# Four small matmuls in TensorE's first waits, and a recomposed work list, in a fused attention and SwiGLU kernel

## The chip, the core and the metric

The kernel runs on one NeuronCore of one Trainium2 chip. The metric is the device time of one execution in microseconds (us); lower is better. Four runs of the kernel before gave 371.88 to 372.51 us with a median of 372.19 us.

## What is computed

Attention over 8 batches of 8 heads, 576 positions of width 64, with 16 extra "beacon" keys and values per head ahead of the ordinary ones. Its output, with the heads side by side, is the input of a SwiGLU feed-forward block on 4608 tokens.

```python
k_all, v_all = concat([beacon_k, k]), concat([beacon_v, v])    # 592 keys
scores = q @ k_all.T / 8 ; scores[ordinary key later than the query] = -1e9
x = softmax(scores) @ v_all                      # to 4608 x 512
g = x @ w_gate ; val = x @ w_val                 # 512 -> 1536
out = (g * sigmoid(g) * val) @ w_out             # 1536 -> 512, fp32 out
```

Inputs and output are fp32; inside, the operands of TensorE are bf16, and the loads on GpSimd's DMA queue convert as they copy.

## The kernel before

**Attention** goes by batch `b` and pair of heads `m` (4 pairs a batch). For one pair the scores of all keys against all queries are cut into four units, A, B, C and D, of 496, 464, 496 and 208 columns for each of the two heads; a unit's matmuls fill a PSUM tile of the pool `big` (3 buffers, `scores`, L285), ScalarE takes the exponent into the tile `p` (L260), and the causal triangle is cut out in one of three ways. Letter `e` in the work list: GpSimd's affine_select on `p` after the exponent (L268). Letter `d`: a multiplication with a 0/1 tile on VectorE (L264). Letter `s`: a matmul that adds -30000 to the scores on TensorE before the exponent (`mask_on_pe`, L249). Units A, B and D take one such GpSimd or VectorE instruction each, C two; with `s` the number doubles, one for each head. `P` is the product with the values for one head, 15 matmuls (`pv`, L309), and two VectorE instructions that normalise it into `x`.

**Queries and keys** must be transposed. Batch 0 is loaded in another layout and regrouped by copies (`c` on VectorE, `C` on GpSimd), then transposed by TensorE: `K`, `Q` with the copy out of PSUM on VectorE, `k`, `q` with it on ScalarE. Batches 1 and 2 are transposed by TensorE too (`U`, `u`, L228); the later ones by DMA from SyncE's queue (`t`, ten a batch). The attention output of batch 0 is transposed by TensorE (`X`, `x`), that of the others by DMA as soon as a batch's last `P` is issued.

**The feed-forward block** goes by chunks `j` of 512 tokens. `G` is one unit of 128 hidden columns: 8 matmuls of 512 columns (L354), Tanh on ScalarE (L367) and two VectorE instructions (L369, L372). The first three units of chunk 0 are cut into nine parts `g`, so that they can begin before all of batch 0 is there. `F` is one matmul of 512 columns of the output projection (L393; twelve make a tile of 128 tokens, which VectorE copies out and SyncE stores).

**Loads.** `l` issues the next of 125 loads of values, keys and queries in a fixed order (`loads`), `w` the next of 8 weight loads of 384 KB (`weights`: gate and value weights for hidden units 0-2, 3-5, 6-8, 9-11), `o` the next half of `w_out`, 768 KB. All of them go through GpSimd's queue, on the same engine as the masks `e`. Each load uses one of eight semaphores in turn, so that a load is issued only when the eighth before it has landed.

**The work list** `plan` sets the order. It is one long string; every letter calls `piece`, which issues that piece to its engines. An engine executes its own instructions in exactly this order, so a TensorE instruction that waits holds all later matmuls, and a mask that waits on GpSimd holds all later loads. Assertions in `piece` state what a piece needs.

**At the start** VectorE zeroes the first 512 columns of one `p` tile, and TensorE runs 15 matmuls on them into a spare PSUM tile (`warm`, L467: nine of 512 columns, six of 128) while the first loads come in.

Of the kernel before, what the change touches and what calls it, by code (L numbers as in the profile page):

```python
# [14 lines left out]
P = 128  # L15
S = 576
# [4 lines left out]
TOK = 512  # L21
# [38 lines left out]
def kernel(  # L60
# [65 lines left out]
    def load_runs(t, src, h0, h1):  # L126
# [151 lines left out]
    def scores(burst):  # L278

        tiles = [big.tile([P, 2, 512], FP32, name="s_ps", tag="big") for _ in burst]  # L280
        for (b, m, u, mask), ps in zip(burst, tiles):
            for t, col, q0, n in UNITS[u][2]:
                for hh in range(2):
                    r = slice(64 * hh, 64 * hh + 64)
                    nc.tensor.matmul(  # L285
                        ps[:, hh, col : col + n],
                        lhsT=kT[b % 2][r, m, P * t : P * t + P],
                        rhs=qT[b % 2][r, m, q0 : q0 + n],
                        start=mask != "s" or col == 0,
                        stop=mask != "s",  # L290
                    )
            if mask != "s":
                exponent(b, m, u, mask, ps)
# [136 lines left out]

    nc.vector.memset(pt[1][:, 0, 0:TOK], 0.0)
    for eng, t, src in ((nc.sync, first_k, k), (nc.scalar, first_q, q)):
        eng.dma_start(t[:].rearrange("p (h e) -> p h e", h=2), src[0, 0:2].rearrange("h (p i) d -> p h (i d)", i=ROWS))
    nc.sync.dma_start(beacons_in[:], beacon_k[0].rearrange("h j d -> j h d"))
# [28 lines left out]
    def warm(n, cols):  # L465
        for _ in range(n):
            nc.tensor.matmul(  # L467
                idle[:, 0:cols], lhsT=pt[1][:, 0, 0:P], rhs=pt[1][:, 0, 0:cols], start=True, stop=True
            )

    warm(9, TOK)
# [19 lines left out]

    done = dict.fromkeys("SPKQUXgGFltwoc", 0)
    first = [[(0, 0, 2), (1, 0, 2), (0, 2, 3), (1, 2, 3), (2, 0, 2), (2, 2, 3), (0, 3, 4), (1, 3, 4), (2, 3, 4)]]
    parts = [(j, *part) for j in range(len(first)) for part in first[j]]
    units = [(j, f) for j in range(NCH) for f in range((3, 0)[min(j, 1)], NF)]
# [28 lines left out]
    def piece(kind):  # L526
# [48 lines left out]
            projection.pop(0)()  # L575
        elif kind == "o":
            load_wo(n)
        elif kind == "w":
            weights[n]()
        elif kind in "cC":  # L580
# [11 lines left out]
    one_bank = [(outp, "outp")]  # L592
    two_banks = [(outp, "outp"), (att, "att")]
    plan = [
        "lllllllclQkcKeeQcdscwCwKeslcQssQKsswPwPeePPewXee",
        "XPllsPgPxgllPwggXlllgwlgwogggGGllGGGGoGlGulGFddF",
        "lllFFFFUddlllllFlFlFllFlFFUdeFFFPUlddlPFFdeeFFFF",
        "PFllFlFdePeeFFlPuFFlllPdeeFFPueFPFdeFlFFtFUeeFFF",
        "PFlFdeelPFtUePtFFeeFPFdeelFPFlllGllGGPtGtGlllGlG",
        "lllPGlGGGllGllllFlFFltttttedFPlFFteetFFFFtFFeeel",  # L600
        "PFtllFFFFFtPddeFtFPFFltFFledePllFFFFFFdddFllFltF",
        "FltPGGPlGtFllGtlPFGtGGGtGGlPttGllFddFllFFFFFlFdt",
        "eeFFFtFlGFddFPtlFFFFdeeFtFFtFlFFPdleeFFFFlFFFlFP",
        "FFeleldPFFGlGttFtFGFGlFFFFPFFFllldeeFPFtGFFeePFF",
        "FdeetFFFPFlGlGGFtGGlFtPFGGlGFlFllFFFFFPFtFldeePF",
        "FFGPGFFFlFlFlFteeFFFFeteelFPFGlteldFFFFPFFGFFFFG",
        "tFlFGGFFFFFFFPFeeleFFFFPGGtGGFFFteeFFFPlFFtFleed",
        "tFFFGGPGFGtGPlGFFtFFdeFFFFFPFFeeetlPFFtGGGFFFFFF",
        "FFFFPeddFFFFPFFlFdedFFFFFPGGGFFFFFFlFeeFFFFFPeee",
        "FFFFFFPFFFFFFPeedFFFFFFFFFFPdeeFFPGFFFGPGGFGFPFG",  # L610
        "GPFFGFGFGFFGGFFFFFFFFFFFFFGFFFFGFFFFGFGFFFFFFFFF",
        "FFFFFGGFFFFGGGGFFFFGGFFFFFFFFFFFFFGFFGFFFFFGFFFG",
        "FFFFFFFGFFFFFFFGFGFFFFFGFGGFFGFGFFFFFFFFFFFFFFFF",
        "FFFFFFFFFFFFFFFFFFFFFFFFFFFFFFFFFFFFF",
    ]
    for kind in re.findall("[sde]{3}(?![sde](?![sde]))|[sde]{1,2}|.", "".join(plan)):
        piece(kind)
    assert done == dict(S=16 * B, P=8 * B, K=4, Q=4, U=4 * (NPE - 1), X=4 * NPEX, g=9, G=len(units), F=4 * NF * NCH, w=8, o=2, c=6, l=len(loads), t=len(turns)), done


# [28 lines left out]
```

The softmax here doesn't subtract the row's maximum and nothing guards it: scores larger than these inputs give would overflow.

## Time and profile before

| | |
|---|---|
| median of four runs | 372.19 us |
| the profiled execution's own time | 371.94 us |
| its span | 370.2 us |
| TensorE busy (matmuls) | 358.3 us, 97% |
| VectorE, ScalarE, GpSimd busy | 241.0, 171.3, 149.6 us |
| TensorE idle before a named wait of over 0.15 us | 1.3 + 1.3 + 0.9 + 0.8 + 0.4 + 0.4 + 0.3 + 0.2 + 0.2 us and 0.7 us of "issue" |

The span starts at 0 with the first instruction of the program; the time beside it has 1.74 us more. A matmul of 512 columns starts 0.216 us after the one before (eight in 1.73 us), though the row of one says 379 ns: the rows overlap, because matmuls are pipelined. "Idle before, and releaser" tells how long the engine had nothing to do before an instruction and what ended that. PEclk is the share of TensorE's full clock that was granted.

### The profile page before, as it was taken

The page shows a single profiled execution, that of the slowest core. Times are in us where ns is not written, and L with a number is a line of the kernel's source. Part 1 is how long each engine was busy: PE and PEld are TensorE (multiplying, and loading weights), DVE is VectorE, ACT ScalarE, POOL GpSimd, SP SyncE. Part 2 cuts the span into 40 slices and gives each one's busy share as a digit, 9 for nine tenths or more (in the row PEclk, how much of TensorE's full clock was granted, in tenths as well). Part 3 has the DMA queues.
Part 4 walks back from the last instruction along what each step waited for, and adds up shares of the span by engine and source line. Part 5 has one row for each costly group of instructions (what it writes and reads, how often), then busy time and mean ns, then how long its engine had stood idle before and what let it go on. Part 6 is the DMA issues. An engine that isn't in the chain of part 4 may idle for free.

```text
span 370.2 us, 7227 instructions
## 1 busy us (share of the span) xinstructions
PE 358.3 (97%) x2792; PEld 180.7 (49%) x2839; DVE 241.0 (65%) x474; ACT 171.3 (46%) x245; POOL 149.6 (40%) x251
## 2 busy tenths in 40 slices
PE   7998999999989999999999999999999999999996
PEld 3663455654444445454454444544555444444443
DVE  5758776768746875666855766767367746656662
ACT  3853379953475258464265454544642311311210
POOL 8987479886768515828045212121310000000000
PEclk9699999999999999999999999999999999999999
DMA  9999999999999999999949178136200301001003
GB/s 167 131 187 176 200 171 154 112 168 115 153 120 162 164 170 138 154 187 92 171 63 109 48 110 120 40 52 93 81 30 0 92 31 57 2 29 57 30 30 112
DMA packets 160978, 39.61 MB, mean 107 GB/s; under 512 B 149040, under 2 KB 156464, under 8 KB 160944
## 3 DMA queue, kind: packets, MB, share of 16 engines
q0 software_dynamic: 112304, 18.83, 73.1%
q1 hardware_dynamic: 48432, 20.02, 27.8%
q8 instruction: 22, 0.36, 0.4%
q10 hardware_dynamic: 208, 0.29, 0.3%
q14 instruction: 12, 0.10, 0.1%
HBM read 38.27 MB, written 9.44 MB: 129 GB/s over the span
## 4 chain that ended last, share of the span: by engine, by line
PE 79%; DMA 12%; POOL 3%; issue 2%; ACT 1%; DVE 1%; POOLq 0%; ACTq 0%
PE gv_ps L354 42%; PE o_ps L393 22%; PE pv_ps L309 6%; PE s_ps L285 6%; DMA qb<-in_q_dram 4%; DMA wo<-in_moe_w_out_dram 3%; DMA wg<-in_moe_w_gate_dram 2%; DMA vb<-in_v_dram 1%; POOL qb L137 1%; ACT p L260 1%; DMA first_k<-in_k_dram 1%; POOL kb L137 1%; PE t_ps L204 1%; PE o_ps L413 1%; PE t_ps L228 1%
## 5 line engine op out<-in xcount | busy, mean ns | idle before, releaser
L367 ACT ACTIVATE th<-gv_ps 128x512 f32<-128x512 f32 x108 | 64.4, 597 | 150.7 <-PE gv_ps L354 138.2
L260 ACT ACTIVATE p<-s_ps 128x992 bf16<-128x992 f32 (+2 forms) x128 | 101.8, 865 | 28.2 <-PE s_ps L285 26.4
L369 DVE SCALAR_TENSOR_TENSOR u<-th,gv_ps 128x512 f32<-128x512 f32 x108 | 74.2, 687 | 62.1 <-ACT th L367 60.6
L354 PE MATMUL gv_ps<-xT,wg 128*128 128x512 bf16 x419 | 110.5, 379 | 2.1 <-DVE hT L372 1.3
L354 PE MATMUL gv_ps<-xT,wv 128*128 128x512 bf16 x425 | 111.0, 379 | 0.4
L393 PE MATMUL o_ps<-wo,hT 128*128 128x512 bf16 x393 | 103.8, 380 | 1.7 <-issue 0.5
L372 DVE SCALAR_TENSOR_TENSOR hT<-gv_ps,u 128x512 bf16<-128x512 f32 x108 | 74.7, 691 | 3.7
L268 POOL TENSOR_SCALAR_AFFINE_SELECT p<-p 128x256 bf16<-128x256 bf16 (+2 forms) x101 | 37.4, 395 | 97.9 <-ACT p L260 91.9
L354 PEld LDWEIGHTS <-wv 128*128 128x128 bf16 x432 | 42.2, 98 | 51.1 <-DMA wv<-in_moe_w_val_dram 0.4
L354 PEld LDWEIGHTS <-wg 128*128 128x128 bf16 x432 | 41.2, 98 | 47.8 <-issue 1.7
L393 PEld LDWEIGHTS <-hT 128*128 128x128 bf16 x420 | 37.2, 98 | 44.0 <-issue 7.0
L309 PEld LDWEIGHTS <-p 128*128 128x128 bf16 x960 | 36.5, 97 | 13.3 <-DVE x L318 1.4
L309 PE MATMUL pv_ps<-vb,p 128*128 128x65 bf16 x960 | 39.9, 193 | 1.4 <-DMA vb<-in_v_dram 0.9
L137 POOL DMA_DIRECT2D vb<-in_v_dram x40 | 34.1, 862 | 9.1 <-DMA qb<-in_q_dram 6.0
L285 PE MATMUL s_ps<-qT,kT 64*128 64x80 bf16 (+4 forms) x384 | 34.0, 290 | 0.8 <-DMA qT<-qb 0.3
L318 DVE TENSOR_TENSOR x<-pv_ps,rec 128x320 bf16<-128x320 f32 x64 | 31.5, 492 | 2.3
L137 POOL DMA_DIRECT2D qb<-in_q_dram x35 | 30.2, 863 | 4.9 <-PE gv_ps L354 2.2
L137 POOL DMA_DIRECT2D kb<-in_k_dram x35 | 30.0, 858 | 4.4 <-DMA wo<-in_moe_w_out_dram 1.7
L402 DVE COPY o_sb<-o_ps 128x512 f32<-128x512 f32 x35 | 24.0, 685 | 10.4 <-PE o_ps L393 10.3
L264 DVE TENSOR_TENSOR p<-p,upper 128x256 bf16<-128x256 bf16 (+2 forms) x49 | 13.7, 296 | 22.5 <-ACT p L260 22.2
L285 PEld LDWEIGHTS <-kT 64*128 64x128 bf16 x384 | 14.1, 95 | 18.5 <-issue 11.4
L317 DVE RECIPROCAL rec<-pv_ps 128x5 f32<-128x5 f32 x64 | 12.1, 189 | 15.7 <-PE pv_ps L309 15.5
(55 smaller groups left out, 84.5 us busy)
## 6 DMA issues: line engine op xcount, KB each, us to landing
out_dram<-o_sb SPq DMA_DIRECT2D x35, 256.0 KB, 2.2
qb<-in_q_dram POOLq DMA_DIRECT2D x28, 128.0 KB, 7.3
vb<-in_v_dram POOLq DMA_DIRECT2D x24, 128.0 KB, 5.5
kb<-in_k_dram POOLq DMA_DIRECT2D x21, 128.0 KB, 6.7
wg<-in_moe_w_gate_dram POOLq DMA_DIRECT2D x4, 384.0 KB, 7.9
wv<-in_moe_w_val_dram POOLq DMA_DIRECT2D x4, 384.0 KB, 9.0
wo<-in_moe_w_out_dram POOLq DMA_DIRECT2D x2, 768.0 KB, 12.8
vb<-in_v_dram POOLq DMA_DIRECT2D x8, 112.0 KB, 5.2
```

Source lines behind the costliest of these rows:

```text
L137: return eng.dma_start(dst[p0 : p0 + n, c, h0:h1, 0:D], src[b, h0:h1, r : r + n, :].rearrange("h j d -> j h d"))
L260: nc.scalar.activation(p[:, :, c0 : c0 + w], ps[:, :, 0:w], ACT.Exp, scale=0.125)
L268: nc.gpsimd.affine_select(out=ap, in_=ap, compare_op=ALU.is_ge, fill=0.0, base=d, pattern=[[0, 2], [1, n]], channel_multiplier=-1,)
L285: nc.tensor.matmul(ps[:, hh, col : col + n], lhsT=kT[b % 2][r, m, P * t : P * t + P], rhs=qT[b % 2][r, m, q0 : q0 + n], start=mask != "s" ...
L309: nc.tensor.matmul(o_ps[:, c, 0 : D + 1], lhsT=pt[(NPAIR * b + m) % NPT][:, hh, col : col + P], rhs=vb[b % 2][:, t, h, 0 : D + 1], start=( ...
L318: nc.vector.tensor_tensor(out=xs[b][:, :, D * h : D * h + D], in0=o_ps[:, :, 0:D], in1=rec[:].to_broadcast([P, NKT, D]), op=ALU.mult,)
L354: nc.tensor.matmul(gvs[f][:, TOK * half : TOK * half + TOK], lhsT=w[:, kk, P * f : P * f + P], rhs=xT[:, kk, r : r + TOK], start=(kk == 0) ...
L367: nc.scalar.activation(th[:], ps[:, 0:TOK], ACT.Tanh, scale=0.5)
L369: nc.vector.scalar_tensor_tensor(out=u[:], in0=th[:], scalar=1.0, in1=ps[:, 0:TOK], op0=ALU.add, op1=ALU.mult)
L372: nc.vector.scalar_tensor_tensor(out=hTs[j][:, f, :], in0=ps[:, TOK:1024], scalar=0.5, in1=u[:], op0=ALU.mult, op1=ALU.mult)
L393: nc.tensor.matmul(st["o"][:], lhsT=hTs[j][:, f, P * i : P * i + P], rhs=wo[:, f, :], start=(f == 0), stop=(f == NF - 1),)
L402: nc.vector.tensor_copy(o_sb[:], st["o"][:])
```

## The change

- A new letter `h`, four times in the list. While at most two score units have been issued it is a `warm` matmul of 256 columns into the spare PSUM tile; later it is remembered in `heat` and issued at the head of the next burst of scores, into that burst's own first tile, ahead of its first score matmul, which overwrites it. Three of the four are of the first kind, one of the second.
- The zeros lie in `p` tile 2 instead of 1.
- The whole list is another one. It has the same pieces with these differences: for batch 0's first pair the two transposes are `q`, `k` (both copied out by ScalarE) and the second pair's keys too (`k`), where it was `Q`, `k`, `K`; all six regroupings are on VectorE (one was on GpSimd).
- The masks: 28 matmuls on TensorE (20 before), 60 instructions on VectorE (49), 86 on GpSimd (101).
- The loads of weights and inputs interleave otherwise: the first gate weights go out right behind batch 1's first key block, the second half of `w_out` ahead of batch 1's values, and so on.

```diff
@@ -129,6 +129,7 @@
             src[0, h0:h1].rearrange("h (p i) d -> p h (i d)", i=ROWS),
         )
 
+    heat = []
     loaded = {}
 
     def rows(eng, dst, src, b, h0, h1, c, p0, r, n):
@@ -278,6 +279,11 @@
     def scores(burst):
 
         tiles = [big.tile([P, 2, 512], FP32, name="s_ps", tag="big") for _ in burst]
+        while heat:
+            heat.pop()
+            nc.tensor.matmul(
+                tiles[0][:, 0, 0 : 2 * P], lhsT=pt[2][:, 0, 0:P], rhs=pt[2][:, 0, 0 : 2 * P], start=True, stop=True
+            )
         for (b, m, u, mask), ps in zip(burst, tiles):
             for t, col, q0, n in UNITS[u][2]:
                 for hh in range(2):
@@ -430,7 +436,7 @@
 
 
 
-    nc.vector.memset(pt[1][:, 0, 0:TOK], 0.0)
+    nc.vector.memset(pt[2][:, 0, 0:TOK], 0.0)
     for eng, t, src in ((nc.sync, first_k, k), (nc.scalar, first_q, q)):
         eng.dma_start(t[:].rearrange("p (h e) -> p h e", h=2), src[0, 0:2].rearrange("h (p i) d -> p h (i d)", i=ROWS))
     nc.sync.dma_start(beacons_in[:], beacon_k[0].rearrange("h j d -> j h d"))
@@ -465,7 +471,7 @@
     def warm(n, cols):
         for _ in range(n):
             nc.tensor.matmul(
-                idle[:, 0:cols], lhsT=pt[1][:, 0, 0:P], rhs=pt[1][:, 0, 0:cols], start=True, stop=True
+                idle[:, 0:cols], lhsT=pt[2][:, 0, 0:P], rhs=pt[2][:, 0, 0:cols], start=True, stop=True
             )
 
     warm(9, TOK)
@@ -491,7 +497,7 @@
 
 
 
-    done = dict.fromkeys("SPKQUXgGFltwoc", 0)
+    done = dict.fromkeys("SPKQUXgGFltwoch", 0)
     first = [[(0, 0, 2), (1, 0, 2), (0, 2, 3), (1, 2, 3), (2, 0, 2), (2, 2, 3), (0, 3, 4), (1, 3, 4), (2, 3, 4)]]
     parts = [(j, *part) for j in range(len(first)) for part in first[j]]
     units = [(j, f) for j in range(NCH) for f in range((3, 0)[min(j, 1)], NF)]
@@ -575,6 +581,12 @@
             projection.pop(0)()
         elif kind == "o":
             load_wo(n)
+        elif kind == "h":
+            assert done["S"] < 8
+            if done["S"] <= 2:
+                warm(1, 2 * P)
+            else:
+                heat.append(1)
         elif kind == "w":
             weights[n]()
         elif kind in "cC":
@@ -592,29 +604,30 @@
     one_bank = [(outp, "outp")]
     two_banks = [(outp, "outp"), (att, "att")]
     plan = [
-        "lllllllclQkcKeeQcdscwCwKeslcQssQKsswPwPeePPewXee",
-        "XPllsPgPxgllPwggXlllgwlgwogggGGllGGGGoGlGulGFddF",
-        "lllFFFFUddlllllFlFlFllFlFFUdeFFFPUlddlPFFdeeFFFF",
-        "PFllFlFdePeeFFlPuFFlllPdeeFFPueFPFdeFlFFtFUeeFFF",
-        "PFlFdeelPFtUePtFFeeFPFdeelFPFlllGllGGPtGtGlllGlG",
-        "lllPGlGGGllGllllFlFFltttttedFPlFFteetFFFFtFFeeel",
-        "PFtllFFFFFtPddeFtFPFFltFFledePllFFFFFFdddFllFltF",
-        "FltPGGPlGtFllGtlPFGtGGGtGGlPttGllFddFllFFFFFlFdt",
-        "eeFFFtFlGFddFPtlFFFFdeeFtFFtFlFFPdleeFFFFlFFFlFP",
-        "FFeleldPFFGlGttFtFGFGlFFFFPFFFllldeeFPFtGFFeePFF",
-        "FdeetFFFPFlGlGGFtGGlFtPFGGlGFlFllFFFFFPFtFldeePF",
-        "FFGPGFFFlFlFlFteeFFFFeteelFPFGlteldFFFFPFFGFFFFG",
-        "tFlFGGFFFFFFFPFeeleFFFFPGGtGGFFFteeFFFPlFFtFleed",
-        "tFFFGGPGFGtGPlGFFtFFdeFFFFFPFFeeetlPFFtGGGFFFFFF",
-        "FFFFPeddFFFFPFFlFdedFFFFFPGGGFFFFFFlFeeFFFFFPeee",
-        "FFFFFFPFFFFFFPeedFFFFFFFFFFPdeeFFPGFFFGPGGFGFPFG",
-        "GPFFGFGFGFFGGFFFFFFFFFFFFFGFFFFGFFFFGFGFFFFFFFFF",
-        "FFFFFGGFFFFGGGGFFFFGGFFFFFFFFFFFFFGFFGFFFFFGFFFG",
-        "FFFFFFFGFFFFFFFGFGFFFFFGFGGFFGFGFFFFFFFFFFFFFFFF",
-        "FFFFFFFFFFFFFFFFFFFFFFFFFFFFFFFFFFFFF",
+        "lllllllclchqwkhhkescQdshcKcelseQcwKswQelswPPdweP",
+        "PessXXlsPPwwgPxllllglPglgwXggglggoGGGGGGGoGlulll",
+        "lGFdldFFFFllFUllddlFlFlFFUesFFPdldllFlFlePlUeFFP",
+        "ddslFPFFFleeFPFFFllsPlUFPFleeFPtltUdFFFlFddeFFtl",
+        "FPtUeeFFPUdelFPltFdlFFFFPFtdelllFltFFPddelttlFll",
+        "lFPlGGllGGGGPGGltPGlGGGFFlleelFtltFFtFFeetFltFll",
+        "llFFFlllleeeFFlFFtFFFedtlFFFlFeeFGGllGPFFFlGtFFP",
+        "GGPtGeeFFFlPlltlFFFFeelePFFGtPGlFFdetFFFFFtPFddl",
+        "elFFPGGltPGFddFFFFFPtlddeFFlFlllFttPFFeeePFFFFtF",
+        "FdedFFtFFGlGtFGtPlFGlGlPlGeeFFFPtFFtlFdeteFPFFtF",
+        "ddFlFlGtltGlGlFtFFGGFlFFFFFFlFFetePlGGFFFeelFFFF",
+        "FFPdtdeFFFGFPFFGFedlFFPFFFledeFFPFGtPFFGFGlGPFFl",
+        "tGFFFFFFtFGlPFFFlllFFFFdedFFFFFGPGGFttFFFeeFFPFe",
+        "eelPFFFFFGeePFFFFFFtttFFdddFFFlFtGtGlGFFFFPGPFFF",
+        "FFFFFGdeFFFFFFPlFFdedPFFlGGFGFGGGlFFeeFFFFFFFPFF",
+        "FedePFFFFFFFedeFFFFPFGPGFFFFFFFPFeddFFFFPGGPGFFF",
+        "FFFPFFFGGGFFFGGGGFFFFFFFFFFFFGFFFFGFFGFGFFFFGFFF",
+        "GFFGFFGFFFFFFGFFFFGGFGFFFFFFFFFFFGFFFFFGFFFFFGFF",
+        "FFFFFGFFFGFFGFGFGFFFFFFGFFFFFFFGFFGFFGFFFFFFFFFF",
+        "FFFFFFFFFFFFFFFFFFFFFFFFFFFFFFFFFFFFFFFFF",
     ]
     for kind in re.findall("[sde]{3}(?![sde](?![sde]))|[sde]{1,2}|.", "".join(plan)):
         piece(kind)
+    del done["h"]
     assert done == dict(S=16 * B, P=8 * B, K=4, Q=4, U=4 * (NPE - 1), X=4 * NPEX, g=9, G=len(units), F=4 * NF * NCH, w=8, o=2, c=6, l=len(loads), t=len(turns)), done
 
 
```

## The prediction

> **What bounds the kernel.** I read the page's busy times first, then TensorE's waits, then the clock by stretches.
>
> ```profile
> PE 358.3 (97%) x2792; PEld 180.7 (49%) x2839; DVE 241.0 (65%) x474; ACT 171.3 (46%) x245; POOL 149.6 (40%) x251
> ...
> PE gv_ps L354 <- DVE hT L372: 1.3, 1, 1.3
> PE idle_ps L467 <- DVE p L433: 1.3, 1, 1.3
> PE pv_ps L309 <- DMA vb<-in_v_dram: 0.9, 2, 0.6
> PE t_ps L204 <- DVE qb L193: 0.8, 1, 0.8
> ...
> PE o_ps L393 <- DMA wo<-in_moe_w_out_dram: 0.4, 1, 0.4
> PE t_ps L201 <- DVE qT L193: 0.4, 1, 0.4
> ...
> ```
>
> TensorE is the bound: a microsecond saved anywhere else counts only if TensorE waited for it. All its named waits come to 6.5 us, so the prize is small. The second place to look is how fast TensorE ran while it was busy.
>
> ```profile
> core 0: us, PE busy (x) PEld busy (x) DVE busy (x) ACT busy (x) POOL busy (x), PEclk, DMA share, GB/s
> ...
> 4.73:8.14 3.41, 2.25 (x30) 1.53 (x30) 2.54 (x7) 1.52 (x4) 3.27 (x7) 1.00 1.29 189
> 8.14:11.55 3.41, 3.41 (x31) 1.85 (x29) 2.48 (x7) 3.02 (x4) 3.41 (x6) 0.50 2.06 158
> 11.55:14.97 3.42, 3.42 (x33) 2.21 (x29) 2.04 (x6) 2.79 (x5) 3.42 (x6) 0.50 1.86 113
> ...
> ```
>
> From 8.14 to 14.97 us the granted clock was half. The stretch before it holds the two waits at 5.41 us (0.77) and 7.15 us (0.39), which is where three of the four new matmuls go.
>
> **Part 1: the four matmuls.** A 512-column matmul takes 0.216 us from start to start at full clock, so 256 columns take 0.11, 0.21 at half clock. One lies in the 0.77 us wait for the query regrouping, two (0.22) in the 0.39 us wait for the first query copy: hidden, cost 0. Without that cover they would cost 0.33. The fourth stands in the second wave of scores, with no wait named before it: 0.1 to 0.2 us, taken as 0.1.
>
> **Part 2: does the clock stay up?** At most, half of the 6.83 us at half clock comes back, 3.4 us, but ScalarE caps it. Its rows:
>
> ```profile
> 7.19 0.72 ACT L191 ACTIVATE kT<-t_ps 128x16 bf16<-128x16 bf16 x2 [1.15 <-PE t_ps L204]
> 8.53 3.14 ACT L260 ACTIVATE p<-s_ps 128x992 bf16<-128x992 f32 x4 [0.62 <-PE s_ps L285]
> 11.92 1.83 ACT L260 ACTIVATE p<-s_ps 128x992 bf16<-128x992 f32 x2 [0.25 <-PE s_ps L285]
> 14.14 1.41 ACT L260 ACTIVATE p<-s_ps 128x416 bf16<-128x416 f32 x2 [0.38 <-PE s_ps L249]
> 16.16 6.22 ACT L260 ACTIVATE p<-s_ps 128x992 bf16<-128x992 f32 x8 [0.62 <-PE s_ps L249]
> ```
>
> Batch 0's exponents are 12.6 us of work and end at 22.38. The last three gaps between them (0.25 + 0.38 + 0.62 = 1.25 us) are all that a faster TensorE can close. Against that, the second pair's key copy (0.72, as the row at 7.19) now stands on ScalarE ahead of the first exponent. By my order: queries' copy 6.66 to 7.32 (0.66, the ScalarE row of 576 columns), keys' to 8.04, second keys' to 8.76; the first exponent starts at 8.76 instead of 8.53, 0.23 late. Kept clock: 1.25 - 0.23 = 1.0 us earlier at best. Lost clock: 0.2 late.
>
> Here the Trainium skill is to be weighed ("TensorE: Matmul & The Clock Gate", Part 1): the gate looks at windows of about 3.4 us, a busy one opens it, an idle one halves the clock. The windows are here (3.41 us each). But the stretch at 4.73 was busy for 2.25 of 3.41 us and closed the gate all the same, and the one at 8.14 was recorded as busy throughout and did not open it. The page's Part 4 says that transposes don't count as busy in the same way; with that, what counts in the stretch at 4.73 is the tail of the warm-up alone, about 0.5 us, and the three matmuls make 0.85. By the general rule (a gap below 3.4 us keeps the clock) the gain would be 1.0; by the row, that a nearly full stretch did not open it, nothing. The page also says that the windows run free, so that their place may differ from run to run. I take 0.4 us of gain, nearer to the middle than to either end, and keep -1.0 to +0.2.
>
> A second cap: hidden unit 9 of chunk 0 needs the last value weights. They were issued at 31.8 us and landed 9.2 us later, at 41.0; TensorE started those matmuls at 41.06. In both lists this load has the same loads ahead of it, so TensorE can't be earlier there than the queue is. GpSimd's rows show room:
>
> ```profile
> 12.20 0.89 POOL L268 TENSOR_SCALAR_AFFINE_SELECT p<-p 128x224 bf16<-128x224 bf16 x2
> 13.04 0.77 POOL L166 DMA_DIRECT2D wg<-in_moe_w_gate_dram  x1
> 13.80 0.84 POOL L193 COPY kb<-ks 96x768 bf16<-96x768 bf16 x1
> 14.57 0.76 POOL L166 DMA_DIRECT2D wv<-in_moe_w_val_dram  x1
> ```
>
> Two masks and a copy stand between the loads, and from 14.5 to 15.5 us only 30 GB/s moved, against 141 to 195 around it. The new list sends the first gate weights at 12.2 and has the copy on VectorE; up to 0.8 us earlier landings follow. So 0.4 is allowed.
>
> **Part 3: the late waits.**
>
> ```profile
> 49.53 0.81 PE L393 MATMUL o_ps<-wo,hT 128*128 128x512 bf16 x3 [0.41 <-DMA wo<-in_moe_w_out_dram]
> ...
> 99.56 0.37 PE L285 MATMUL s_ps<-qT,kT 64*128 64x464 bf16 x2 [0.34 <-DMA qT<-qb]
> ...
> 104.75 0.31 PE L309 MATMUL pv_ps<-vb,p 128*128 128x65 bf16 x5 [0.64 <-DMA vb<-in_v_dram]
> 105.31 0.19 PE L309 MATMUL pv_ps<-vb,p 128*128 128x65 bf16 x1 [0.24 <-DMA vb<-in_v_dram]
> ```
>
> *w_out.* Its second half was issued at 36.1, behind a beacon block and one block of batch 1's values, and landed at 49.5. Now only the beacon block is ahead; landings in this stretch are 0.65 to 0.9 us apart, so it lands about 0.7 earlier, at 48.8, where TensorE asked from 49.1. Gain 0.4. The values behind it end where they did (52.9), and the first `P` of batch 1 asks at 52.6 for its first block: no slack to spare, but no new load.
>
> *Transposed queries of batch 3.* I laid both lists out in TensorE's own work (G 1.73, F 0.216, P 0.56, a pair's scores about 0.7 us). Before, the last five DMA transposes stood directly ahead of batch 3's first scores. Now the last one stands 8 us ahead; one took 6.5 us to land at 92 us. Gain 0.34. What its data need, batch 3's last query block, was issued at 81.7; its letter now comes 3 us earlier.
>
> *Values of batch 3.* The first `P` stood 4 us behind the letter of the last value block, now 10 us. That block landed 4.9 us after its issue at 100.4. Gain 0.64 + 0.24 = 0.88.
>
> Sum: 1.6 us. The 1.27 us wait for hT at 28.5 stays: three units still finish together.
>
> **Part 4: masks.** TensorE: 8 more matmuls. Their row gives 271 ns of one, but four from 20.93 on were followed by the next group at 21.12: 0.05 each, 0.1 at half clock. Cost 0.4 to 0.8, taken as 0.4. VectorE: 11 more at 0.29 = 3.2 us on an engine busy 65%; hidden, since TensorE waits for VectorE nowhere in the attention stages by more than 0.2. GpSimd: 15 fewer at 0.40 = 6 us out of the queue that issues the loads. A rule against the change is in "SBUF: State Buffer", the section on two separate sides: a VectorE instruction with two SBUF inputs locks a GpSimd one that reads SBUF out, for its whole length. By it, 11 x 0.29 us of lock, on GpSimd busy 40%: up to 1.3 us of its time; by the rows (101 masks of 0.32 to 0.55 us, 0.41 the median) the spread is small, and the 6 us freed outweigh it. Taken as 0.
>
> **Part 5: new waits.** So much is reordered that something will be late that was not. The old list had six named waits of 0.15 us or more after 30 us that are no "issue", 2.0 us in all (wo, qT and vb twice, and two of 0.2 for a mask and a copy); I charge 0.3, with 0 to 2.5 for the range.
>
> Sum: 0.1 - 0.4 - 1.6 + 0.4 + 0.3 = -1.2. Against the profiled execution: 371.94 - 1.2 = **370.7 us**; that execution is 0.25 below the median shown, so by the median it is 1.5 less.
>
> **Rivals.** A change of under 0.2% (0.74 us, so 371.45 to 372.93) is about what a measurement of this kernel can't tell from none.
>
> *The clock falls as before.* Three short matmuls are too little; the start loses 0.2 instead of gaining 0.4: 371.3. For it: the stretch at 8.14 stayed slow at full recorded load.
>
> *The waits only move.* TensorE arrives earlier and meets the same queue: loads kept the DMAs busy until about 185 us (twenty slices of 9 on the page), and each landing has its time. Then part 3 gives back what it gains, 1.2 or so, and the time is 371.9. Against it: the two waits near 100 us go because TensorE's order changes.
>
> *Slower: loads behind a mask.* The last three blocks of batch 2's keys and queries were issued at 54.4 to 56.0 and the last landed at 61.3, while TensorE transposed that batch from 60.80 to 61.56: no slack. Their letters now stand behind a GpSimd mask of pair 1 of batch 1, which waits for ScalarE's exponent (that exponent ran at about 52 to 53 us). If GpSimd is free by 53.5, as I work it out, nothing is lost, since TensorE's list has 1.1 us more ahead of the transposes. Each later microsecond is one on TensorE; from 2 us on, landing at 63.3 or later, it outweighs the 1.2, and 3.2 us, which a late ScalarE could make (it is busy 89% from 60 to 70 us), gives 373.9; 2.7 us gives 373.4.
>
> **Chances.** Waits go and the start gains something: 0.45, range of its own 369.9 to 371.3. Clock falls: 0.20, split at 371.45 as 0.15 and 0.05. Waits only move: 0.15, of which 0.02 is faster and 0.02 slower. Slower by the mask or a wait like it: 0.20, of which 0.04 is within 0.2%. So faster 0.62, same 0.20, slower 0.18. The range takes in the bounds of parts 2 and 4 below and most of the slow case above: 369.4 to 373.2.
>
> **What would show it.** Right: no wait for `vb` or `qT` near 100 us, none for `wo` near 49, PEclk above 0.5 between 8.14 and 14.97, ScalarE's last exponent of batch 0 before 22. Wrong: the clock at 0.5 with the 41 us mark unmoved, or a wait of TensorE of over 0.5 us for `qb`, `kb` or `vb` between 50 and 70 us.

## The result, and the profile after

The changed kernel takes **370.67 us** (median of 43 runs, 369.94 to 372.99) against 371.92 us for the kernel before (64 runs, 370.18 to 376.50). The ratio is 0.9966, with a 95% interval of 0.9956 to 0.9977: 1.25 us faster, where the prediction had 370.7 us and 1.2 us. The profiled execution took 370.37 us with a span of 368.7 us, against 371.94 and 370.2, so the two traces differ by 1.5 us of span.

The page's busy times of the changed kernel first, then its list of TensorE's waits (us in total, times, longest us).

```profile
PE 357.6 (97%) x2805; PEld 180.0 (49%) x2851; DVE 242.3 (66%) x485; ACT 170.6 (46%) x246; POOL 143.4 (39%) x235
```

```profile
PE gv_ps L360 <- DVE hT L378: 1.3, 1, 1.3
PE idle_ps L473 <- DVE p L439: 1.3, 1, 1.3
PE o_ps L399 <- issue: 1.0, 6, 0.2
PE s_ps L291 <- ACT p L261: 0.9, 3, 0.4
PE gv_ps L360 <- DMA wv<-in_moe_w_val_dram: 0.8, 1, 0.8
PE t_ps L205 <- DVE qb L194: 0.3, 1, 0.3
```

The waits for `vb`, `wo` and `qT` are gone from the list. New are 0.8 us for value weights and three short waits for ScalarE's exponents, 0.9 us in all. (The changed file has six more lines, so L354, L393, L285 and L309 of before are L360, L399, L291 and L315 here.)

The clock by stretches in the changed kernel; after the stretch and its length come the busy times of PE, PEld, DVE, ACT and POOL with their instruction counts, then the granted TensorE clock, the DMA share and GB/s.

```profile
4.73:8.14 3.41, 3.35 (x31) 2.27 (x29) 1.94 (x6) 2.13 (x6) 3.27 (x7) 1.00 1.31 197
8.14:11.55 3.41, 3.02 (x36) 1.71 (x37) 1.77 (x4) 3.41 (x7) 3.41 (x6) 1.00 1.79 138
11.55:14.97 3.42, 2.75 (x39) 1.68 (x36) 3.42 (x9) 3.42 (x6) 3.42 (x7) 1.00 1.94 131
```

From 8.14 to 14.97 us the clock is now full where it was half. The first row needs care: it holds 3.35 us of TensorE work where it held 2.25, but its 1.00 is not a full clock. The trace's record of the clock begins at 7.24 us with the first full-speed window, and the column says 1.00 ahead of a record too. Ahead of 7.24 TensorE ran at half speed, as two groups of six like transposes show (start, us, instruction):

```profile
6.03 0.66 PE L205 MATMUL t_ps<-ident,qb 96*128 96x96 bf16 x6
```

```profile
7.65 0.43 PE L205 MATMUL t_ps<-ident,kb 96*128 96x96 bf16 x6
```

In the trace before, the full clock came at 4.73 us already and was lost at 8.14. So part of the 3.35 us is the same work done at half speed, and this trace alone does not show what the four matmuls do. The last section comes back to that.

ScalarE follows at once. Its timeline in the changed kernel (idle before and releaser at the end of a row):

```profile
8.72 9.30 ACT L261 ACTIVATE p<-s_ps 128x992 bf16<-128x992 f32 x12
18.21 3.13 ACT L261 ACTIVATE p<-s_ps 128x992 bf16<-128x992 f32 x4 [0.19 <-PE s_ps L291]
```

The first exponent starts at 8.72 (the prediction worked out 8.76), and batch 0's exponents end at 18.21 + 3.13 = 21.34 instead of 22.38. That is 1.04 us earlier, all that the prediction said ScalarE allowed. What TensorE made of it is in its own timeline in the changed kernel:

```profile
20.68 0.38 PE L360 MATMUL gv_ps<-xT,wg 128*128 128x512 bf16 x1
21.91 0.60 PE L360 MATMUL gv_ps<-xT,wv 128*128 128x512 bf16 x2 [0.85 <-DMA wv<-in_moe_w_val_dram]
...
48.86 1.04 PE L399 MATMUL o_ps<-wo,hT 128*128 128x512 bf16 x4
...
98.70 0.58 PE L291 MATMUL s_ps<-qT,kT 64*128 64x496 bf16 x4
```

At 21.06 TensorE is ready for the first value weights and has them only at 21.9. The wait for hT, which ends at 29.67, is as long as before (1.27 us). At 48.86 the output projection finds `w_out` there, where it started at 49.53 after a wait, and the scores at 98.70 find their transposed queries.

To see where the 1.5 us lie I took both spans in the same stretches (columns as above) and read TensorE's idle time as length minus busy time. First the kernel before, then the changed one:

```profile
4.73:14.97 10.24, 9.08 (x90) 5.59 (x88) 7.06 (x17) 7.33 (x12) 10.10 (x17) 0.67 1.73 153
14.97:30.00 15.03, 13.65 (x203) 8.86 (x205) 9.77 (x25) 9.12 (x13) 12.46 (x20) 1.00 1.50 172
30.00:78.40 48.40, 46.98 (x492) 26.07 (x499) 34.75 (x80) 32.69 (x45) 36.10 (x61) 1.00 1.68 160
78.40:113.00 34.60, 33.01 (x268) 16.29 (x272) 23.69 (x44) 18.15 (x26) 26.63 (x40) 1.00 2.00 137
```

```profile
4.73:14.97 10.24, 9.11 (x104) 5.66 (x102) 7.13 (x17) 8.96 (x16) 10.10 (x18) 1.00 1.68 155
14.97:30.00 15.03, 12.79 (x196) 8.67 (x197) 8.94 (x24) 8.51 (x12) 12.23 (x19) 1.00 1.48 185
30.00:78.40 48.40, 47.37 (x513) 26.59 (x519) 36.31 (x90) 31.48 (x42) 36.32 (x54) 1.00 1.88 164
78.40:113.00 34.60, 34.23 (x216) 15.89 (x218) 23.20 (x39) 17.87 (x26) 22.58 (x35) 1.00 1.72 153
```

Idle goes from 1.16 to 1.13, from 1.38 to 2.24, from 1.42 to 1.03 and from 1.59 to 0.37. So the start lost 0.83 us more to waiting, and the stretch from 30 to 113 us lost 1.61 less (0.39 + 1.22). Over the whole span idle fell by 0.8 (370.2 - 358.3 to 368.7 - 357.6), so outside these stretches nothing changed on balance. Busy time fell by 0.7 although the new list has about 0.86 us more to do (four matmuls of 256 columns at 0.108, eight masks of 128 at 0.054, both by the 0.216 us of 512 columns). The remainder, some 1.5 us, I put down to the clock. It is a residual, and a few matmul records can be missing from a trace. An estimate from the clock itself is larger, 2.2 us: half of the difference between 6.83 us at half speed before and 2.51 us (4.73 to 7.24) after.

### The profile page after: what moved, and what is told of

The parts are those of the page before. It is cut to its first block, busy times and chain, and to the rows that moved or that the text cites. A ratio compares the mean times of both kernels' runs of the same rounds, so it can differ in the third digit from the quotient of the medians.

```text
span 368.7 us, 7251 instructions
## 1 busy us (share of the span) xinstructions
PE 357.6 (97%) x2805; PEld 180.0 (49%) x2851; DVE 242.3 (66%) x485; ACT 170.6 (46%) x246; POOL 143.4 (39%) x235
## 4 chain that ended last, share of the span: by engine, by line
PE 90%; POOL 4%; DMA 2%; issue 1%; DVE 1%; ACT 1%; POOLq 0%
PE gv_ps L360 50%; PE o_ps L399 24%; PE pv_ps L315 7%; PE s_ps L291 6%; DMA wv<-in_moe_w_val_dram 2%; POOL vb L138 1%; PE t_ps L229 1%; PE o_ps L419 1%; POOL kb L138 1%; ACT p L261 0%; DVE u L375 0%; POOL qs L127 0%; ACT th L373 0%; POOL ks L127 0%; POOL p L269 0%
## 5 line engine op out<-in xcount | busy, mean ns | idle before, releaser
L360 PE MATMUL gv_ps<-xT,wv 128*128 128x512 bf16 x427 | 111.1, 379 | 1.2 <-DMA wv<-in_moe_w_val_dram 0.8
L360 PE MATMUL gv_ps<-xT,wg 128*128 128x512 bf16 x416 | 110.0, 379 | 2.1 <-DVE hT L378 1.3
L399 PE MATMUL o_ps<-wo,hT 128*128 128x512 bf16 x395 | 105.4, 380 | 1.7 <-issue 1.0
L269 POOL TENSOR_SCALAR_AFFINE_SELECT p<-p 128x256 bf16<-128x256 bf16 (+2 forms) x86 | 32.9, 410 | 112.3 <-ACT p L261 109.6
L360 PEld LDWEIGHTS <-wv 128*128 128x128 bf16 x432 | 42.2, 98 | 51.8 <-DMA wv<-in_moe_w_val_dram 1.1
L360 PEld LDWEIGHTS <-wg 128*128 128x128 bf16 x432 | 41.0, 98 | 47.3 <-issue 1.6
L399 PEld LDWEIGHTS <-hT 128*128 128x128 bf16 x420 | 36.9, 98 | 42.4 <-issue 5.9
L315 PEld LDWEIGHTS <-p 128*128 128x128 bf16 x960 | 36.2, 97 | 13.2 <-DVE x L324 1.9
L315 PE MATMUL pv_ps<-vb,p 128*128 128x65 bf16 x960 | 39.2, 193 | 0.1
L265 DVE TENSOR_TENSOR p<-p,upper 128x256 bf16<-128x256 bf16 (+2 forms) x60 | 16.2, 291 | 29.4 <-ACT p L261 29.2
L291 PE MATMUL s_ps<-qT,kT 64*128 64x80 bf16 (+4 forms) x384 | 33.1, 281 | 1.2 <-ACT p L261 0.9
L138 POOL DMA_DIRECT2D kb<-in_k_dram x35 | 30.8, 879 | 3.0 <-DMA wo<-in_moe_w_out_dram 2.8
L291 PEld LDWEIGHTS <-kT 64*128 64x128 bf16 x384 | 14.0, 94 | 20.4 <-issue 15.6
```

What stands on the lines that cost most here:

```text
L138: return eng.dma_start(dst[p0 : p0 + n, c, h0:h1, 0:D], src[b, h0:h1, r : r + n, :].rearrange("h j d -> j h d"))
L269: nc.gpsimd.affine_select(out=ap, in_=ap, compare_op=ALU.is_ge, fill=0.0, base=d, pattern=[[0, 2], [1, n]], channel_multiplier=-1,)
L291: nc.tensor.matmul(ps[:, hh, col : col + n], lhsT=kT[b % 2][r, m, P * t : P * t + P], rhs=qT[b % 2][r, m, q0 : q0 + n], start=mask != "s" ...
L315: nc.tensor.matmul(o_ps[:, c, 0 : D + 1], lhsT=pt[(NPAIR * b + m) % NPT][:, hh, col : col + P], rhs=vb[b % 2][:, t, h, 0 : D + 1], start=( ...
L360: nc.tensor.matmul(gvs[f][:, TOK * half : TOK * half + TOK], lhsT=w[:, kk, P * f : P * f + P], rhs=xT[:, kk, r : r + TOK], start=(kk == 0) ...
L399: nc.tensor.matmul(st["o"][:], lhsT=hTs[j][:, f, P * i : P * i + P], rhs=wo[:, f, :], start=(f == 0), stop=(f == NF - 1),)
```

## The experiments

The theory: the late waits were landings that TensorE's order had met too early, and the new list moved them out of the way. The rivals: the four matmuls with the clock make the gain; or landings simply move, and a list that comes earlier waits longer. Each time below is a median of 12 runs (5 for the last) to be set against the kernel before on the same chip: 372.02 us (35 runs) for the first four, 372.08 (29 runs) for the others. Of each list only the first row or rows that an edit touches are shown. Where letters were added or taken out, those behind are the same and only move across the row breaks.

**1. The old list with the four matmuls.**

Besides the lines here it has the code of the letter `h` from the change.

```diff
-    nc.vector.memset(pt[1][:, 0, 0:TOK], 0.0)
+    nc.vector.memset(pt[2][:, 0, 0:TOK], 0.0)
-        "lllllllclQkcKeeQcdscwCwKeslcQssQKsswPwPeePPewXee",
+        "lllllllclhQkchhKeeQcdshcwCwKeslcQssQKsswPwPeePPe",
```

> The old list with the four small matmuls alone (zeros in p tile 2; one before the first query transposes, two before the second key transposes, one after the first pair's scores). Theory (the queue of loads caps the start): the clock stays up, ScalarE's last exponent of batch 0 ends some 1.0 us earlier than 22.4, but chunk 0's unit 9 still starts its value matmuls when the last value weights land, about 41.0 us, so the time moves by -0.3 to +0.3 us. Rival (the kept clock is the gain): 0.9 to 1.3 us faster, the 41 us mark moves to 40.2 or earlier.

Measured: 371.94 us, ratio 0.9991 (0.9964 to 1.0018). Nothing that can be told from zero. The runs differ by their clock: the median is 371.54 us for the seven in which it held and 372.93 for the five in which it fell. The trace is of the slowest of the twelve (374.24 us), with two falls. It shows what a faster start meets in the old list, in its TensorE row, its GpSimd row and its ScalarE rows:

```profile
14.82 0.66 PE L205 MATMUL t_ps<-ident,kb 96*128 96x96 bf16 x6 [1.32 <-POOL kb L194]
```

```profile
13.93 0.84 POOL L194 COPY kb<-ks 96x768 bf16<-96x768 bf16 x1
```

```profile
16.73 3.22 ACT L261 ACTIVATE p<-s_ps 128x992 bf16<-128x992 f32 x4 [2.33 <-PE s_ps L250]
20.22 3.23 ACT L261 ACTIVATE p<-s_ps 128x992 bf16<-128x992 f32 x4 [0.27 <-PE s_ps L291]
```

In this execution the clock was full from 4.24 to 14.48 us. TensorE came to the next pair's keys at 13.5 and had to wait 1.32 us for the regrouping that GpSimd does behind the gate weights' issue. Then the clock fell, for 3.41 us. ScalarE stood idle for 2.33 us over both, and the exponents ended at 23.45, later than before (22.38). So the theory's time held, but its picture did not: the first wall was not the last value weights but the regrouping on GpSimd, just behind the slow stretch. The new list has that copy on VectorE.

**2. The new list without the four matmuls.**

```diff
-        "lllllllclchqwkhhkescQdshcKcelseQcwKswQelswPPdweP",
+        "lllllllclcqwkkescQdscKcelseQcwKswQelswPPdwePPess",
```

> The new list without its four small matmuls, nothing else changed. Theory: the granted clock falls to half for 3 to 7 us after about 8 us, the exponents of batch 0 end 0.7 to 1.2 us later than in the new kernel, and the 0.85 us wait for the first value weights at 21 us swallows most of it: 0 to 0.4 us slower than the new kernel, so 0.8 to 1.3 us faster than before. Rival (the kept clock is the gain): the gain is gone, within 0.3 us of before. Second rival: the clock does not fall, the order of the transposes keeps it up, and nothing changes at the start.

Measured: 370.66 us, ratio 0.9962 (0.9932 to 0.9992), as fast as the changed kernel by the median. The list makes the gain of the median, not the four matmuls. They do something that a median hides. Sorted by the granted clock of each run, here 6 of 12 runs had it fall somewhere (their median 371.98 us) and 6 did not (370.46); of the changed kernel's 44 runs with a clock on record (one more than its median takes), 2 had it fall. Means over all runs are 371.21 and 370.88. So with the matmuls the clock stays up in nearly every run, and in this list a fall goes with 1.5 us. In the kernel before, runs whose clock fell were slower by only 0.16 us on the one chip (20 of 35 fell; medians 372.11 and 371.95) and 0.30 on the other (17 of 29). So the list and the clock need each other. Where the clock held, the list alone brings 371.95 us (27 runs before) down to 370.46. Where it fell, it brings 372.19 (37 runs) only to 371.98, a difference that six runs can't tell from nothing. The one trace of this variant is of a run in which the clock held, so where it falls in the others isn't known.

That trace shows ScalarE without a gap (timeline):

```profile
8.75 12.47 ACT L261 ACTIVATE p<-s_ps 128x992 bf16<-128x992 f32 x16
```

In it TensorE has no wait for the first value weights, and the first Tanh of chunk 0 starts at 26.96 us, against 27.57 in the changed kernel's trace, though these weights were issued at 14.89 and 14.97. The landing itself differs from one execution to another: this load took 6.4 us from issue to landing here, 6.9 in the changed kernel's trace and 7.5 in experiment 4's, where the wait was 1.08 us.

**3. The old list up to the end of chunk 0's hidden units, then the new one.** The first two rows of the new list, with the four `h`, are replaced by the first two of the old; one pair of input loads evens out the counts at the seam.

```diff
-        "lllllllclchqwkhhkescQdshcKcelseQcwKswQelswPPdweP",
-        "PessXXlsPPwwgPxllllglPglgwXggglggoGGGGGGGoGlulll",
+        "lllllllclQkcKeeQcdscwCwKeslcQssQKsswPwPeePPewXee",
+        "XPllsPgPxgllPwggXlllgwlgwogggGGllGGGGoGlGulGllFd",
```

> The old list up to the last unit of chunk 0's first 12, the new list from the first projection matmul on (the two value loads that fall between the cuts issued at the seam), no small matmuls. Theory: the waits for transposed queries and values near 100 us are gone, the wait for w_out near 49 us is there: 0.5 to 1.1 us faster than before. Rival (the start brings the gain): within 0.3 us of before.

Measured: 371.70 us, ratio 0.9976 (0.9955 to 0.9998), 0.9 us faster than before, with an interval just clear of no change. The waits near 100 us are gone. The one for `w_out` is there, in TensorE's timeline:

```profile
49.47 1.02 PE L399 MATMUL o_ps<-wo,hT 128*128 128x512 bf16 x4 [0.42 <-DMA wo<-in_moe_w_out_dram]
```

Set against the changed kernel's trace it is level to 40 us, 0.12 later at 42 us, 0.59 later at the first output copy (51 us), 1.35 later at the first Tanh of chunk 1 (78 us), and 1.35 to the end. Three waits in between are named: 0.42 for `w_out`, 0.18 for values at 53.0 and 0.19 for a GpSimd mask at 60.3. So what the changed start is worth falls due only behind chunk 0's first units, from 40 us on, where its order has brought loads in earlier; the earlier exponents as such give nothing there. The waits named make 0.79 of the 1.35; the rest I can't place.

**4. The new start, then the old list.**

```diff
-        "lGFdldFFFFllFUllddlFlFlFFUesFFPdldllFlFlePlUeFFP",
+        "lGFddFlFFFFUddlllllFlFlFllFlFFUdeFFFPUlddlPFFdee",
```

> The new list up to the last unit of chunk 0's first 12, with its small matmuls, the old list from the first projection matmul on. Theory: the start is 0.2 us earlier at its end and the w_out wait of 0.41 us is gone, the waits near 100 us are as before: 0.3 to 0.8 us faster than before. Rival (the rest brings all): within 0.2 us. Rival (the start brings all): 1.0 to 1.3 us faster.

Measured: 371.40 us, ratio 0.9984 (0.9952 to 1.0016): 0.6 us faster, as expected, but not to be told from no change. Here the waits for batch 3's values are back (TensorE's timeline):

```profile
104.98 0.31 PE L315 MATMUL pv_ps<-vb,p 128*128 128x65 bf16 x5 [0.38 <-DMA vb<-in_v_dram]
105.51 0.19 PE L315 MATMUL pv_ps<-vb,p 128*128 128x65 bf16 x1 [0.22 <-DMA vb<-in_v_dram]
```

This execution (372.24 us, slower than the median) also waited 1.08 us for the first value weights and 0.78 for the transposed attention output at 77.5 us; I don't know why the latter came late. It is useful all the same. At the first Tanh of chunk 1 it was 1.07 us behind the kernel before, and from the first Tanh of chunk 2 (116 us) on only 0.20. So 0.87 us of lateness vanished over the stretch with the landings near 100 us: the waits for the values are 0.28 us shorter than before (0.60 for 0.88), and the 0.34 us wait for the transposed queries did not occur. Whoever comes later waits less there. By the same wall, what is won ahead of it would be paid back; that was not tried by itself.

**5. The old list with two of its waits removed by hand.** Batch 3's last five DMA transposes go ahead of four hidden units, three output matmuls and nine loads, and its first three products with the values eight, four and four output matmuls later.

```diff
-        "lllPGlGGGllGllllFlFFltttttedFPlFFteetFFFFtFFeeel",
-        "PFtllFFFFFtPddeFtFPFFltFFledePllFFFFFFdddFllFltF",
+        "lllPGtttttlGGGllGllllFlFFledFPlFFteetFFFFtFFeeel",
+        "FtllFFFFFtddeFtFPFFPltFFPledePllFFFFFFdddFllFltF",
```

> The old kernel with two edits: the last five DMA transposes of batch 3 stand six units of the feed-forward block earlier, and the first three head products of batch 3 stand 6 to 12 projection matmuls later. No small matmuls, same masks, same loads. Theory (the landing of batch 3's values near 105 us is a wall that swallows whatever was gained before it): both waits near 100 us are gone, 0.7 to 1.3 us faster than before, and now the runs with a full clock are at least 0.3 us faster than those where the clock fell. Rival (the waits only move): within 0.3 us of before. Second rival (the queue near 49 us is the wall): 0.2 to 0.5 us faster, no difference by clock.

Measured: 373.11 us, ratio 1.0022 (1.0006 to 1.0038): slower by 0.8 us (0.0022 of 372). The waits for queries and values are gone, and TensorE's timeline shows what stands in their place:

```profile
105.95 0.37 PE L285 MATMUL s_ps<-qT,kT 64*128 64x464 bf16 x2 [0.51 <-ACT p L260]
...
108.20 0.62 PE L309 MATMUL pv_ps<-vb,p 128*128 128x65 bf16 x15 [0.45 <-DVE x L318]
...
109.73 0.62 PE L309 MATMUL pv_ps<-vb,p 128*128 128x65 bf16 x15 [0.47 <-POOL p L268]
...
111.16 0.62 PE L309 MATMUL pv_ps<-vb,p 128*128 128x65 bf16 x15 [0.20 <-DVE x L318]
```

That is 1.63 us for the 1.22 removed (0.34 + 0.88). The scores no longer have products between them while ScalarE takes their exponents, and the products then come one behind the other, faster than VectorE normalises and GpSimd masks. The 0.7 to 1.3 us that I expected did not come, and the rival that waits only move is right for this edit, which did worse than that. (Runs whose clock held are 0.35 us faster than those in which it fell, as expected, but they are only seven and five.) The new list gets rid of the same waits without these, because the order of score units, products and output matmuls around them is another one as well. In this execution the clock, once full at 7.24 us, did not fall either, and it still reached its first Tanh at 27.77 (27.64 before), after 0.99 us for the same GpSimd copy as in experiment 1.

**6. The new list with the gate and value weights earlier.** The first two weight loads go out right behind batch 0's values, the last value weights right behind the last gate weights. A product of batch 1 (`P`) is also moved, past two VectorE masks, three loads and an output matmul.

```diff
-        "lllllllclchqwkhhkescQdshcKcelseQcwKswQelswPPdweP",
-        "PessXXlsPPwwgPxllllglPglgwXggglggoGGGGGGGoGlulll",
-        "lGFdldFFFFllFUllddlFlFlFFUesFFPdldllFlFlePlUeFFP",
+        "llllllwwlclchqkhhkescQdshcKcelseQcKswQelswPPdweP",
+        "PessXXlsPPwwwgPxllllglPglgXggglggoGGGGGGGoGlulll",
+        "lGFdldFFFFllFUllddlFlFlFFUesFFdldllFPlFlePlUeFFP",
```

> The new list with the first gate and value weights ahead of batch 1's first key blocks, the last value weights behind the last gate weights, and batch 1's first head product one projection matmul later. Theory (the first value weights' landing at 21.9 us is the wall that swallows the kept clock): no wait for wv at 21 us, the first tanh of chunk 0 is 0.6 to 0.9 us earlier (26.7 to 27.0 us), 0.4 to 0.9 us faster than the new kernel. Rival (the next landing, w_out at 47.3 or batch 1's values at 51.6, takes its place): the tanh is earlier, the end is not, within 0.2 us of the new kernel.

Measured: 372.29 us, ratio 0.9992 (0.9969 to 1.0016): the gain of the new list is lost, where 0.4 to 0.9 us more was expected. The first half of the edit did its work: no wait for the weights, first Tanh at 26.63 instead of 27.57, and still 0.94 us ahead at 51 us. So the 0.85 us wait is what held the start. The other half undid it. TensorE's row, and VectorE's:

```profile
54.56 1.01 PE L315 MATMUL pv_ps<-vb,p 128*128 128x65 bf16 x15 [1.74 <-DVE x L324]
```

```profile
52.95 0.92 DVE L265 TENSOR_TENSOR p<-p,upper 128x256 bf16<-128x256 bf16 x3 [1.59 <-ACT p L261]
53.80 0.18 DVE L323 RECIPROCAL rec<-pv_ps 128x5 f32<-128x5 f32 x1
```

The moved product's normalisation now stands behind VectorE masks that wait 1.59 us for ScalarE's exponent; the next product needs that normalisation, and TensorE stands for 1.74 us. The clock fell right after it, from 54.23 to 57.65. Against the changed kernel the trace goes from 0.94 ahead to 1.47 behind at 55.4 us, where batch 2's next keys are transposed, and to 2.35 behind from 60 us to the end. The load order alone, without the moved product, was not tried.

**7. The same with chunk 0's first units in another order of parts**, so that they don't all end together.

```diff
-    first = [[(0, 0, 2), (1, 0, 2), (0, 2, 3), (1, 2, 3), (2, 0, 2), (2, 2, 3), (0, 3, 4), (1, 3, 4), (2, 3, 4)]]
+    first = [[(0, 0, 2), (1, 0, 2), (0, 2, 3), (1, 2, 3), (2, 0, 2), (0, 3, 4), (1, 3, 4), (2, 2, 3), (2, 3, 4)]]
```

> The same, and the third unit's third part stands behind the last parts of the first two units, so that the first unit is done 0.43 us earlier and the 1.27 us wait for hT shrinks to about 0.84. Theory: another 0.3 to 0.45 us, 0.7 to 1.3 us faster than the new kernel. Rival (a landing takes its place): no faster than the kernel without this edit.

Measured: 371.65 us, ratio 0.9994 (0.9973 to 1.0014), again no gain over the kernel before. The wait for hT shrank from 1.27 to 0.84 us, as expected. But here the rival, that the next landing takes the place of the first, came true in part. The first Tanh is 0.79 us ahead of the changed kernel's and the first output copy only 0.41; between them TensorE waits for `w_out` again:

```profile
48.47 1.02 PE L399 MATMUL o_ps<-wo,hT 128*128 128x512 bf16 x4 [0.33 <-DMA wo<-in_moe_w_out_dram]
```

It has the same wait for the moved product (1.42 us at 54.88) and is 1.47 us behind the changed kernel from 60 us on. Its clock didn't fall there, which is likely why it is 2.35 - 1.47 = 0.88 us nearer than experiment 6.

**8. The new list with all of GpSimd's masks on VectorE.** Every `e` becomes `d`: 70 letters, 86 mask instructions.

```diff
-        "lllllllclchqwkhhkescQdshcKcelseQcwKswQelswPPdweP",
+        "lllllllclchqwkhhkdscQdshcKcdlsdQcwKswQdlswPPdwdP",
```

> The new list with every mask that GpSimd had (86 instructions) on VectorE instead; nothing else. Theory (a mask costs by what queues behind it): VectorE gets 86 x 0.29 = 25 us more, 72% busy, hidden on the whole, but each mask waits for ScalarE's exponent and holds the copies and the two hT instructions behind it, so TensorE waits for hT and qT: 0.3 to 2.5 us slower than the new kernel. Rival (VectorE has room, and loads no longer queue behind masks): within 0.3 us or up to 0.5 us faster. Rival (GpSimd and VectorE block each other on a shared port): L269's going away makes VectorE's own instructions shorter, L265's mean below 0.27 us.

Measured: 378.34 us, ratio 1.0166 (1.0137 to 1.0195), 7.4 us slower than the changed kernel by the two ratios (0.0200 of 372). The direction was expected, the size not. Its largest wait and its group of masks (durations in ns, least, median, most):

```profile
PE pv_ps L315 <- DVE x L324: 2.9, 6, 1.0
```

```profile
L265 DVE TENSOR_TENSOR p<-p,upper x146: 234/284/294, 9.7 to 281.8; 128x256 bf16<-128x256 bf16 x86, 128x224 bf16<-128x224 bf16 x31, 128x160 bf16<-128x160 bf16 x29
```

VectorE is busy for 259.8 us, 69% of the span, so it isn't the bound by its share. TensorE's waits that name VectorE come to 6.9 us without those for hT and for the warm-up's zeros, which both traces have, where the changed kernel's trace has 0.3; that is most of the 8.9 us between the two traces, and puts the cost on the order. A mask that waits for ScalarE stands ahead of the normalisations, regroupings and copies that TensorE waits for. The trace is 1.8 us behind the changed one at the first Tanh, 5.4 at 78 us and 8.9 from 233 us on (it is the slowest of the five runs, with one fall of the clock at 15.05). The rival of a shared port did not reach its mark: the mean of all masks is 275 ns, not below 270, where it was 291, though the largest form went from 315 to 290. None of these eight versions beats the changed kernel beyond the noise.

## Why the prediction was right, and where it was not

| term | predicted | measured |
|---|---|---|
| start: four matmuls, clock, waits to 30 us | 0.1 - 0.4 = -0.3 | 0.43 - 1.5 + 0.83 = -0.2 |
| waits from 30 to 113 us, old and new | -1.6 + 0.3 = -1.3 | -1.61 |
| eight more masks on TensorE | +0.4 | +0.4 (worked out, not measured apart) |
| sum | -1.2 | -1.4 by these terms, -1.5 by the spans |

The 1.5 in the first row is the residual from above, so the last column adds up to the spans by construction. The marks of the two traces give the start between 0.07 us, at the first Tanh, and 0.19, at chunk 0's last.

**The late waits: right, and in the traces they are most of the gain.** All four went, and the stretches show 0.39 + 1.22 = 1.61 us less idle. The 0.3 us that I charged for new waits did not come net: what remains there is "issue" of at most 0.2 us apiece and one exponent of 0.2. Experiments 3 and 4 tie the waits to the parts of the list: near 100 us they go with the new rest, the one for `w_out` with the new start. The measured times can't divide the gain: 0.9 us for the new rest alone and 0.6 for the new start alone, with intervals of 0.8 and 1.2 us to either side. The second half of `w_out` was issued at 35.1 and landed at 47.3, 2.2 us earlier than before; I had 0.7 and a landing at 48.8, which would just have done for the matmuls at 48.86.

**The start: the sum was right by luck, one step of it false.** A larger saving by the clock than my 0.4 us met 0.83 us of waiting that I did not have. The cap by ScalarE was 1.0 us, and the exponents do end 1.04 earlier. The step that failed is the "second cap". I named the last value weights, landing at 41.0, and gave up to 0.8 us of earlier landings. They did land earlier, at 39.7, and nothing waited for them; that took the lead from 0.07 to 0.19 us. The **first** value weights were the cap: issued at 14.97 instead of 14.57, landed at 21.86 instead of 21.36. I had read that GpSimd's queue had room (too freely: the half microsecond ahead of the dip to 30 GB/s moved 90, not 141) and didn't follow the first value weights through it: between the gate weights and these, the new order has three masks and a key block where the old one had a single copy (GpSimd's timeline in the changed kernel):

```profile
12.29 0.81 POOL L167 DMA_DIRECT2D wg<-in_moe_w_gate_dram  x1
13.06 0.77 POOL L269 TENSOR_SCALAR_AFFINE_SELECT p<-p 128x224 bf16<-128x224 bf16 x2
13.71 0.95 POOL L138 DMA_DIRECT2D kb<-in_k_dram  x1
14.61 0.48 POOL L269 TENSOR_SCALAR_AFFINE_SELECT p<-p 128x256 bf16<-128x256 bf16 x1
14.97 0.82 POOL L167 DMA_DIRECT2D wv<-in_moe_w_val_dram  x1
```

Hence 1.04 us earlier on ScalarE is 0.07 at the first Tanh (27.57 for 27.64) and 0.19 at chunk 0's last (46.13 for 46.32). Experiment 6 shows it from the other side: weights earlier, start 0.94 earlier. How long this wait is varies with the landing: none, 0.85 and 1.08 us in the three traces with this order of loads (experiments 2 and 4 and the changed kernel).

**The clock: right that it stays up, wrong about what a fall costs.** I took the lost clock as 0.2 us. That fits the old list, where a fall goes with 0.16 to 0.30 us and experiments 1 and 5 show GpSimd's copy as the next wall. In the new list's variant without the four matmuls a fall goes with 1.5 us. So the rival "the clock falls as before", 371.3, looks priced too low: those runs have a median of 371.98. It is not settled, since only two of the six have a clock as low as a fall at the start leaves it.

What makes the clock fall is not settled either. The Trainium skill ("TensorE: Matmul & The Clock Gate", Part 1) lets the clock fall after an idle window of about 3.4 us; its Part 4 says that transposes don't count as busy in the same way, and I leaned on that to explain a fall after 2.25 us of work in 3.41. The last section has a fall with no transpose ahead of it.

**The rivals.** "The waits only move" did not decide this change, but it is real: experiments 4 and 5 show it for the old list. The slower rival, batch 2's last query block behind a GpSimd mask, did not happen: that block was issued at 54.99 and landed at 60.59, before 61.3. **Masks on VectorE** at nothing: no wait of TensorE names VectorE between 30 and 113 us, so 11 more were covered, and so were two more transposes of batches 1 and 2 that copy on VectorE alone (`U`, seven for five; the old waits for VectorE of 0.77 and 0.39 us lay ahead of the first of these masks). Experiment 8 puts the limit to it: at 86 more the cover is gone. The lock between the two engines shows as single long masks on VectorE: 610 ns at most in the changed kernel, 481 before, 294 with no mask on GpSimd. In the changed kernel all four above 294 ns ran beside a GpSimd mask, and together they are 0.9 us longer than that, as the six before are: no difference, as taken.

## What to carry to other kernels

A landing can be a wall: time won ahead of it is handed back there, as part of it was in experiment 7, until the list itself puts other work in front of it. So follow each load that a changed order passes from its issue to its first user, the earliest one above all, and price a lost clock with the next wall in mind, since a fall went with 0.2 or 0.3 us in one order and with 1.5 us in another. When one wait is taken away by moving a piece, look at what VectorE and GpSimd now have behind one another; in both tries by hand (experiments 5 and 6) the new wait was larger than the one removed.

## What the runs showed of the hardware that was not expected

The clock falls in windows far from idle. It is granted in windows of 3.41 us whose place differs from run to run. TensorE starts at half speed (in every trace the first matmuls of 512 columns start 0.427 us apart), and full speed comes at 4.73 us in the trace before, at 7.24 after, at 5.28 in experiment 7. These are the windows ahead of a fall in experiments 1 (two) and 6, and one in experiment 7 after which it held; columns as in the stretches above.

```profile
11.06:14.48 3.42, 2.03 (x31) 1.34 (x29) 2.98 (x6) 3.35 (x5) 3.42 (x6) 1.00 2.02 129
103.22:106.64 3.42, 2.01 (x28) 1.21 (x23) 0.75 (x3) 2.72 (x3) 2.28 (x7) 1.00 1.75 142
```

```profile
50.82:54.23 3.41, 1.56 (x26) 0.86 (x21) 1.78 (x6) 3.40 (x5) 3.41 (x5) 1.00 2.33 169
```

```profile
53.07:56.48 3.41, 1.98 (x30) 1.26 (x31) 2.20 (x8) 1.80 (x4) 3.41 (x5) 1.00 2.02 190
```

The six falls ahead of the last few microseconds in the traces of all versions followed windows with 1.56 to 2.25 us of recorded TensorE work, 46 to 66% of the window. No window with 2.30 us or more was followed by one. Some with 1.98 to 2.15 us were not either, the one of experiment 7 and the one with the hT wait (2.14 us in the changed kernel), so between 2.0 and 2.3 the recorded busy time doesn't decide. Nor do transposes: the window at 103.22 has none on TensorE and lost the clock, the one at 53.07 has ten and kept it. In experiment 1 that window also tells the price where little hides it: across the values' waits and the fall that followed, the trace went from 0.5 to 2.3 us behind the kernel before. Of these 1.8 us, 0.53 are longer waits for values (1.41 for 0.88).

**The four small matmuls do keep the clock up at the start.** Two traces have the old start and full speed from nearly the same moment, experiment 1 with the matmuls and experiment 3 without. These are their first windows at full speed:

```profile
4.24:7.65 3.41, 2.51 (x31) 1.60 (x30) 2.60 (x6) 1.39 (x4) 3.27 (x8) 1.00 1.27 191
```

```profile
4.30:7.72 3.42, 2.21 (x29) 1.49 (x27) 2.72 (x6) 1.51 (x4) 3.28 (x8) 1.00 1.28 196
```

They differ by 0.30 us of work, about the three matmuls of 0.108 us that lie there. The first kept the clock until 14.48 us, the second lost it at 7.72 for two windows, as the trace before did. Experiment 8, with the matmuls, has 2.64 us in such a window from 4.81 on and kept it. Where full speed came late, at 6.94 us in experiment 2 and 7.24 in experiment 5, the clock held without the matmuls: the warm-up itself ran at half speed and filled most of the wait behind it (in experiment 2, 0.26 us of it is left, where the kernel before waited 0.77).

The runs say the same. A fall of two windows leaves a mean granted clock of 0.990 (the traces of before and of experiment 3), so I counted the runs at 0.991 or less: 39 of 100 in the four versions without the matmuls, 1 of 97 in the six with them, and that one is experiment 1's trace with its two later falls. So the matmuls remove this fall from the old list and from the new one. Falls of one window remain in both; the four in the traces (experiments 1, 6 and 8) come later, from 14.48 us on. In time they are worth little by themselves: nothing that can be told in the old list (experiment 1), and in the new one 0.3 us of the mean (371.21 to 370.88), which these runs can't tell from nothing.
